# GLU steps on pairs of column blocks that share a 512-column PSUM bank, on one Trainium2 core

## The chip, the core and the metric

The kernel runs on one core of one Trainium2 chip. The engines meant below are TensorE (PE, its weight loads PEld), VectorE (DVE), ScalarE (ACT), GpSimd (POOL) and the DMA queues. The metric is device time in microseconds (us) of one execution. The time before is the median of three runs.

## The reference

```python
def _attn_ref(x):                                   # x [8, 3072, 256]
    return np.fft.fft(np.fft.fft(x, axis=1), axis=2).real.astype(np.float32)

def _moe_ref(x, w_gate, w1, w2):                    # tokens N = 24576, D = 256, E = 8, F = 1024
    # every token goes to one expert, greedily by descending logit, cap N // E tokens each
    ...
    for e in range(E):
        mask = assigned == e
        h = np.maximum(x[mask] @ w1[e], 0.0)
        out[mask] = h @ w2[e]

def _moe2_ref(x, w_a, w_b, w_out):                  # w_a, w_b [256, 1536], w_out [1536, 256]
    return ((x @ w_a) * (x @ w_b) @ w_out).astype(np.float32)
```

The three are chained: the FFT's output goes through the experts, and theirs through the last layer, called the GLU here.

## The kernel before

First comes the FFT over sequence and features (`fft_phase`). Then 48 **superblocks** of 512 tokens run, six per expert. Superblock `sb` starts with eight groups of expert products, `first(f)` into a PSUM tile `mm`, then ACT's `hH`, DVE's `hL`, and `second(f)` into two tiles `acc`. Behind them, in the same superblock, stands the GLU of superblock `sb - 1`. All products use float16 high and low halves, three matmuls for one product.

The GLU writes both `x wa` and `x wb` as Winograd's seven products on halves of features and tokens. Its loop runs over `f` = 0 to 11, blocks of 128 columns. For one `f`:

- `p1` makes tile A (`mm`); ACT copies it twice, to `u` (scaled) and to `w`. `p6` makes tile B (`acc`); DVE adds it to `u`. `p5` makes tile D (`mm`); DVE's `v = w + D`.
- `p2` adds to A; ACT copies it to `c`. `p7` adds to B; DVE's `v += B`. `p3` adds to D; DVE's `u += D`, and POOL's `g[256:] = u * v`.
- `p4`, one round later, adds to B; DVE's `w += B` and `mul`: `g[:256] = c * w`.
- `high` and `low` split `g`, 512 columns, into `gH` (ACT) and `gL` (POOL); `last(f)` multiplies both by `wot` into the tiles `y`. It is written two rounds after `p1(f)`.

Every product has 256 columns (two halves of 128 tokens). Tiles A and D rotate through three PSUM banks `mm`, B through two banks `acc` (for `f` = 0 and 1 it borrows those of `y`). Each engine runs its instructions in the order in which they are written.

Side work is written in between by `tick()` (class `Side`): the routing of the next experts (tiles `cmp`, `rt_...`, products into `bank`), the split of their weights, the preparation of tokens (`prepare`), and the end of `rescale`, which makes `x1H` and `x1L` for the next GLU. A model of the engines' queues (class `Meter`) decides: a step of side work is let in while VectorE's model time is at most 0.48 us (`SLACK`) past TensorE's. The model takes 0.066 us + columns / 960 for a VectorE instruction. Token rows come by `ahead` (an indirect DMA on POOL's queue, tile `xg`), results leave by `finish` (`ysb`, then indirect DMAs).

Almost every instruction is recorded under line L637 of a helper, so the rows are told apart by tiles.

Of the kernel before, what the change touches and what calls it, by code (L numbers as in the profile page):

```python
# [24 lines left out]
F32 = mybir.dt.float32  # L25
F16 = mybir.dt.float16
BF16 = mybir.dt.bfloat16
I32 = mybir.dt.int32
# [22 lines left out]
def shape_constants():  # L51
# [20 lines left out]
    for h in range(2):  # L72
# [23 lines left out]
        np.eye(128),  # L96
# [11 lines left out]
    below = np.stack([t <= t2, (t >= 64) & (t + 64 <= t2)], 1)       # rows t and t + 64 of the prefix sums  # L108
# [20 lines left out]
FEATURES = np.r_[0:128, 255:127:-1]      # feature at each position of a stored row  # L129


# ---------------------------------------------------------------- FFT over sequence and features
def fft_phase(tc, nc, x, wg, cd, xs, L, tick, done):
    """X = Re FFT2(x), by batch. Row n = 32 p + m of x sits on partition p = 2 a + ro, n = 64 a + 32 ro + m.
    First a DFT over a with twiddles (the product also brings the features onto partitions), then the
    DFT over the features on the sums and differences of features d and 256 - d, then the DFT over r."""
    with ExitStack() as ctx:
# [61 lines left out]
        def stage1(b, g):  # L199
            """rows m = 4 g .. 4 g + 3"""  # L200
# [93 lines left out]
# ---------------------------------------------------------------- routing: greedy by logit, with capacities  # L294
class Router:
    """Experts close in the order in which the descending greedy fills them. phase() finds the next
    one: the largest value T at which some open expert has as many unassigned tokens (by their best
    open expert) as it has room for. The search goes over the order-preserving integer image of
    float32, four bits a round. Generators: 'p' comes before tensor-engine work on fresh data."""

    def __init__(s, tc, nc, L, cd, pool, work, psum):
# [7 lines left out]
        sq = const("sq", [128, 4, 128])  # L309
        s.ident, s.samek, s.sel0, s.sel1 = [sq[:, i] for i in range(4)]  # L310
# [15 lines left out]
        s.rhs = []  # L326
        for i in range(2):
            t = pool.tile([128, NT + 4], F16, name=f"rhs{i}")
            nc.vector.tensor_copy(t[:, NT:], s.pcol)
            s.rhs.append(t)  # L330
# [18 lines left out]
    def choose(s, sl, pen=True):  # L349
        """every token's best open expert: the logit, its number, the number as one-hot"""  # L350
# [24 lines left out]
    def count(s):  # L375
        """D: by threshold (and tile) the tokens at or over it, by expert"""
# [37 lines left out]
    def phase(s, number, last):  # L414
        nc = s.nc
        est = s.tmp([128, 1], name="est")          # 8 - expert
# [28 lines left out]
        for r in range(8):  # L445
# [23 lines left out]
            if r == 0:  # L469
                # the bits of the bracket's lower end: of the integer, then of the float it stands for  # L470
# [46 lines left out]
        # the expert's tokens over T, and as many of the ties as it has room for  # L517
# [6 lines left out]
    def compact(s, j, gi, si):  # L524
        """rows to gather (gi) and token numbers (si) of the closing expert's CAP tokens"""
# [3 lines left out]
        for g in range(CAP // 512):  # L529
# [29 lines left out]
            # batch = floor(col / KS), by rounding at 2^23  # L559
# [137 lines left out]
def pow2_scales(nc, work, m, k, inv, scale):  # L697
    """inv = 2^floor(log2 m) * 2^-k, scale = 1/inv: m*scale in [2^k, 2^(k+1))"""
# [11 lines left out]
def fft_moe_glu_kernel(ctx, tc, x, wg, w1, w2, wa, wb, wo, cd, out):  # L710
# [16 lines left out]
    nc.scalar.dma_start(ki, cd["ints"])  # L727

    id16 = keep.tile([128, 128], BF16, name="id16")
    nc.vector.tensor_copy(id16, R.ident)  # L730

    unread = []

# [646 lines left out]
```

## Time and profile before

| | |
|---|---|
| median of three runs | 3851.84 us (3850.18 to 3852.17) |
| span of the profiled execution | 3846.4 us |
| PE busy in it | 3593.1 us, 93% |
| DVE busy | 3168.7 us, 82% |
| POOL busy | 2034.1 us, 53% |
| ACT busy | 1831.1 us, 48% |

The page's times are those of one profiled execution, and its span is the time from its first to its last instruction; the profiled execution has no time of its own beside this span, so the 5.4 us between span and median are taken as what lies around it. A matmul of 256 columns is drawn with some 0.27 us, but the next one starts 0.11 us later: a busy TensorE is not one at its peak, and a short stall behind a matmul doesn't show as idle time.

### The profile page before, as it was taken

The numbers are of one execution on the slowest core, as the hardware profiler recorded it, in microseconds if no ns is written. First come the engines' busy times: TensorE is split into PE (matmuls) and PEld (weight loads), VectorE is DVE, ScalarE is ACT, GpSimd is POOL, SyncE is SP. The second block draws the span as 40 slices with busy tenths as digits, with TensorE's granted clock in tenths as the row PEclk, the third lists the DMA queues.
The fourth block names the chain that finished last, engine by engine and source line by source line (L and its number), as shares of the span: only waits on it lengthen the run. The fifth ranks groups of instructions, "written<-read, shape, count | busy, mean of one in ns | idle before, by whom it ended". The sixth has DMA issues, their size and how long they took to land.

```text
span 3846.4 us, 75545 instructions
## 1 busy us (share of the span) xinstructions
PE 3593.1 (93%) x27819; PEld 2668.8 (69%) x27819; DVE 3168.7 (82%) x7867; ACT 1831.1 (48%) x4590; POOL 2034.1 (53%) x2367
## 2 busy tenths in 40 slices
PE   7998389999999999999999999999999999999998
PEld 7876256766776777667767766767667667776767
DVE  5677889899889988998999899878967797676766
ACT  2444244454445445444544454445455545545544
POOL 3333645654655555555555654655556555555545
PEclk9999599999999999999999999999999999999999
DMA  6665111101011001001100110011010000111000
GB/s 171 164 173 147 34 28 29 40 23 28 19 44 28 20 21 49 21 23 27 43 25 23 44 24 23 23 45 23 23 50 23 26 20 23 29 23 28 23 18 12
DMA packets 183636, 159.67 MB, mean 42 GB/s; under 512 B 110720, under 2 KB 159808, under 8 KB 181216
## 3 DMA queue, kind: packets, MB, share of 16 engines
q1 hardware_dynamic: 132224, 63.45, 7.1%
q0 software_dynamic: 23616, 76.57, 6.1%
q10 hardware_dynamic: 27424, 14.81, 1.8%
q8 instruction: 218, 3.57, 0.4%
q14 instruction: 154, 1.26, 0.1%
HBM read 79.29 MB, written 50.33 MB: 34 GB/s over the span
## 4 chain that ended last, share of the span: by engine, by line
PE 53%; DVE 30%; issue 7%; ACT 5%; POOL 3%; DMA 1%; ACTq 0%; DVEq 0%; POOLq 0%
PE mm L637 18%; PE acc L637 15%; PE y L637 11%; DVE u L637 4%; DVE v L637 4%; DVE g L637 3%; DVE cmp L637 3%; PE u L637 3%; PE bank L637 2%; DVE x1L L637 2%; DVE w L637 2%; ACT gH L637 2%; PE d L637 2%; PE s L637 2%; DVE hL L637 2%
## 5 line engine op out<-in xcount | busy, mean ns | idle before, releaser
L1160 POOL TENSOR_TENSOR gL<-g,gH 128x512 f16<-128x512 f32 x575 | 677.6, 1178 | 866.2 <-ACT gH L637 852.4
L637 PE MATMUL y<-wot,gH 128*128 128x256 f16 x4608 | 847.2, 273 | 2.6 <-ACT gH L637 2.6
L637 PE MATMUL y<-wot,gL 128*128 128x256 f16 x2304 | 629.8, 273 | 35.3 <-POOL gL L1160 33.7
L637 PEld LDWEIGHTS <-wst 128*128 128x128 f16 x5184 | 506.4, 98 | 123.9 <-issue 64.0
L1141 POOL TENSOR_TENSOR g<-u,v 128x256 f32<-128x256 f32 x576 | 454.4, 789 | 252.9 <-DVE u L637 190.8
L637 ACT ACTIVATE c<-mm 128x256 f32<-128x256 f32 x576 | 221.4, 384 | 686.4 <-PE mm L637 683.1
L637 PEld LDWEIGHTS <-gH 128*128 128x128 f16 x4608 | 444.7, 98 | 65.9 <-ACT gH L637 3.6
L637 ACT CAST gH<-g 128x512 f16<-128x512 f32 x577 | 355.7, 617 | 240.2 <-DVE g L637 193.1
L637 PE MATMUL mm<-xT,w1H 128*128 128x512 f16 x1536 | 460.3, 381 | 8.6 <-DMA xT<-xhl 8.6
L637 PE MATMUL mm<-x1H,wat 128*128 128x256 f16 x2304 | 439.7, 273 | 0.0
L637 ACT ACTIVATE hH<-mm 128x512 f16<-128x512 f32 x384 | 228.8, 596 | 408.1 <-PE mm L637 349.6
L637 PEld LDWEIGHTS <-wbt 128*128 128x128 f16 x3456 | 337.1, 98 | 89.1 <-issue 41.8
L637 PEld LDWEIGHTS <-wat 128*128 128x128 f16 x3456 | 336.1, 98 | 89.5 <-issue 2.7
L637 DVE TENSOR_TENSOR g<-c,w 128x256 f32<-128x256 f32 x576 | 365.6, 635 | 6.1
L637 DVE SCALAR_TENSOR_TENSOR hL<-mm,hH 128x512 f16<-128x512 f32 x384 | 262.9, 687 | 127.7 <-ACT hH L637 127.7
L637 PE MATMUL acc<-x1H,wst 128*128 128x256 f16 x1920 | 366.3, 272 | 0.0
L1207 POOL DMA_INDIRECT out_dram<-ysb,si x192 | 202.3, 1054 | 248.4 <-ACT ysb L637 207.6
L637 ACT ACTIVATE u<-mm 128x256 f32<-128x256 f32 x576 | 218.6, 380 | 227.2 <-PE mm L637 225.5
L637 PE MATMUL mm<-x1L,wat 128*128 128x256 f16 x1152 | 314.0, 273 | 0.9 <-ACT w L637 0.7
L637 PE MATMUL acc<-x1L,wst 128*128 128x256 f16 x960 | 261.4, 272 | 43.5 <-DVE u L637 43.5
L637 PEld LDWEIGHTS <-gL 128*128 128x128 f16 x2304 | 224.9, 98 | 107.8 <-POOL gL L1160 78.9
L637 PE MATMUL acc<-hL,w2H 128*128 128x512 f16 x768 | 290.9, 379 | 9.4 <-DVE hL L637 9.2
(241 smaller groups left out, 8338.6 us busy)
## 6 DMA issues: line engine op xcount, KB each, us to landing
xt<-in_x_dram SPq DMA_DIRECT2D x64, 384.0 KB, 5.5
xs<-XO SPq DMA_DIRECT2D x24, 384.0 KB, 3.2
xs<-XO ACTq DMA_DIRECT2D x48, 192.0 KB, 4.9
dwin<-in_moe_w_a_dram POOLq DMA_DIRECT2D x12, 256.0 KB, 4.7
dwin<-in_moe_w_b_dram POOLq DMA_DIRECT2D x12, 256.0 KB, 4.9
dwin<-in_moe_w_out_dram POOLq DMA_DIRECT2D x12, 256.0 KB, 3.3
xg<-xs,gi POOLq DMA_INDIRECT x192, 2.8
out_dram<-ysb,si POOLq DMA_INDIRECT x192, 2.5
```

The source lines that it names most:

```text
L637: r = f(*args, **kw)
L1141: nc.gpsimd.tensor_mul(t["g"][:, 256:], t["u"], t["v"])
L1160: nc.gpsimd.tensor_sub(gL, g, gH)
L1207: st = nc.gpsimd.indirect_dma_start(out=out, out_offset=bass.IndirectOffsetOnAxis(ap=si[:, c:c + 1], axis=0), in_=ysb[:, i], in_offset=None)
```

## The change

The loop runs over `q` = 0 to 5, pairs of column blocks. `products` fills both halves of a 512-column bank, three matmuls each of 256 columns as before, and every copy, sum and product behind it handles 512 columns in one instruction. `u * v` is written back into `u` and `c * w` into `c`. `high` and `low` now split `c` (tiles `gH0`, `gL0`, both blocks, first token half) and `u` (`gH1`, `gL1`) one by one, and `last` takes one token half `h` at a time: half 1 one round after its pair, half 0 two rounds after. `tick()` is called after nearly every step, eleven times in a full round; before, it was five times per `f`. B borrows a bank of `y` for `q` = 0 alone.

```diff
-        def product(self, dst, name, f, start=False):
+        def products(self, dst, name, F, start=False):
             i = self.X[name]
...
+            for n in range(2):
+                for w, v in ((0, self.L), (0, self.H), (1, self.H)):
+                    nc.tensor.matmul(dst[:, n * 256:n * 256 + 256], ab_part(name, w, 2 * F + n), v[:, i], start=start,
+                                     stop=(w == 1), skip_group_check=True)
+                    start = False
...
+        def p1(self, F):
+            t = self.t[F] = {n: ring.tile([128, 512], F32, name=n, bufs=1 if n == "v" else 2) for n in "uvwc"}
+            t["A"] = pmm.tile([128, 512], F32, name="mm", bufs=3)
+            self.products(t["A"], "A11", F, True)
...
-            nc.gpsimd.tensor_mul(t["g"][:, 256:], t["u"], t["v"])
...
+            nc.gpsimd.tensor_mul(t["u"], t["u"], t["v"])
...
-            nc.vector.tensor_mul(t["g"][:, :256], t["c"], t["w"])
...
+            nc.vector.tensor_mul(t["c"], t["c"], t["w"])
...
+            t["H", h] = ring.tile([128, 512], F16, name="gH%d" % h, bufs=2 - h)
+            t["L", h] = ring.tile([128, 512], F16, name="gL%d" % h, bufs=2 - h)
+            nc.scalar.copy(t["H", h], t["cu"[h]])
...
+            (eng or nc.gpsimd).tensor_sub(t["L", h], t["cu"[h]], t["H", h])
...
+        for q in range(6 if G else 0):
+            G.p1(q)
             tick()
...
+            if q == 0 and more:
+                second(6)
+                tick()
+            G.p6(q)
+            if q > 0:
+                G.high(q - 1, 1)
+                G.low(q - 1, 1)
+                tick()
+                G.p4(q - 1)
+                G.mul(q - 1)
+                tick()
+            if q > 1:
+                G.last(q - 2, 0, (0,))
+                tick()
+                G.last(q - 2, 0, (1,))
+                tick()
+            G.p5(q)
+            tick()
...
+            G.p2(q)
             tick()
...
+            if q > 0:
+                G.high(q - 1, 0)
+                G.low(q - 1, 0)
+            G.p7(q)
...
+            if q > 0:
+                G.last(q - 1, 1, (0,))
+                tick()
+                G.last(q - 1, 1, (1,))
+                tick()
+            G.p3(q)
             tick()
```

Around it, small constants change: `ones` is one column that is broadcast, `id16` comes from `ident16` (the float32 identity is no longer loaded), `rhs` of the routing has one buffer, not two, and some one-column tiles have fewer. Comments are removed. The number of matmuls is the same.

Three places show how instructions move. The first is VectorE's queue inside the GLU loop of a late superblock, without side work; before, for one block `f` (twelve of these in a superblock):

```order
L637 SCALAR_TENSOR_TENSOR u<-acc,u 128x256
L637 TENSOR_TENSOR w<-w,acc 128x256
L637 TENSOR_TENSOR v<-w,mm 128x256
L637 TENSOR_TENSOR g<-c,w 128x256
L637 TENSOR_TENSOR v<-v,acc 128x256
L637 SCALAR_TENSOR_TENSOR u<-mm,u 128x256
```

and now, for one pair (six of these):

```order
L634 SCALAR_TENSOR_TENSOR u<-acc,u 128x512
L634 TENSOR_TENSOR w<-w,acc 128x512
L634 TENSOR_TENSOR c<-c,w 128x512
L634 TENSOR_TENSOR v<-w,mm 128x512
L634 TENSOR_TENSOR v<-v,acc 128x512
L634 SCALAR_TENSOR_TENSOR u<-mm,u 128x512
```

Half as many instructions stand there, each of twice the columns, and `c * w` goes back into `c`.

The second is POOL's queue in the part of the GLU loop in which the rows of a later superblock are fetched (`xg`); before:

```order
L1160 TENSOR_TENSOR gL<-g,gH 128x512
L991 DMA xg<-xs,gi 128x256
L1141 TENSOR_TENSOR g<-u,v 128x256
L1160 TENSOR_TENSOR gL<-g,gH 128x512
L991 DMA xg<-xs,gi 128x256
```

and now (`gL` first from `u`, then from `c`):

```order
L1142 TENSOR_TENSOR u<-u,v 128x512
L1162 TENSOR_TENSOR gL_42795<-u,gH_42794 128x512
L1162 TENSOR_TENSOR gL_42834<-c,gH_42833 128x512
L989 DMA xg<-xs,gi 128x256 x2
L1142 TENSOR_TENSOR u<-u,v 128x512
```

Both fetches of a round stand together, between the second `gL` of a pair and the product `u * v` of the next.

The third is VectorE's queue in the GLU loop of a superblock that carries one round of the routing's search (four `cmp`); before:

```order
L637 TENSOR_TENSOR v<-v,acc 128x256
L637 SCALAR_TENSOR_TENSOR u<-mm,u 128x256
L637 TENSOR_TENSOR cmp<-v,rt_th 128x768
L637 SCALAR_TENSOR_TENSOR u<-acc,u 128x256
L637 TENSOR_TENSOR w<-w,acc 128x256
L637 TENSOR_TENSOR v<-w,mm 128x256
L637 TENSOR_TENSOR g<-c,w 128x256
L637 TENSOR_TENSOR v<-v,acc 128x256
L637 SCALAR_TENSOR_TENSOR u<-mm,u 128x256
L637 TENSOR_REDUCE am_31786<-rmx 128x1
L637 TENSOR_TENSOR cmp<-v,rt_th 128x768
```

and now:

```order
L634 SCALAR_TENSOR_TENSOR u<-mm,u 128x512
L634 TENSOR_TENSOR cmp<-v,rt_th 128x768
L634 SCALAR_TENSOR_TENSOR u<-acc,u 128x512
L634 TENSOR_TENSOR w<-w,acc 128x512
L634 TENSOR_TENSOR c<-c,w 128x512
L634 TENSOR_TENSOR cmp<-v,rt_th 128x768
L634 TENSOR_TENSOR v<-w,mm 128x512
L634 TENSOR_TENSOR v<-v,acc 128x512
L634 TENSOR_TENSOR cmp<-v,rt_th 128x768
L634 SCALAR_TENSOR_TENSOR u<-mm,u 128x512
L634 TENSOR_TENSOR cmp<-v,rt_th 128x768
```

All four `cmp` of a round now lie within one pair's steps; before, there was one to a block, and the other two of the round follow in the next two blocks.

Counted over superblocks 1 to 46 in VectorE's queue, 33 superblocks before hold a full load of routing or weight splits, one (number 33) a part, 12 at most two such instructions. Now 28 hold a full load, three a part, and 15 at most two.

## Rows read from the trace of the kernel before

**Rows 1.** The page: the span.

```profile
span 3846.4 us, 75545 instructions
```

**Rows 2.** Stretches: length, busy PE, PEld, DVE, ACT, POOL, clock, DMA share, GB/s.

```profile
498.50:3720.80 3222.30, 3095.43 (x24388) 2266.06 (x24389) 2740.15 (x6871) 1597.66 (x3899) 1762.32 (x2028) 1.00 0.11 28
1286.50:1644.60 358.10, 340.98 (x2750) 249.94 (x2749) 324.96 (x829) 176.14 (x427) 197.56 (x222) 1.00 0.10 29
3260.10:3326.20 66.10, 65.17 (x496) 47.81 (x494) 45.39 (x103) 33.17 (x84) 36.19 (x44) 1.00 0.10 25
3656.70:3720.80 64.10, 64.10 (x495) 48.14 (x493) 42.95 (x103) 33.12 (x84) 32.41 (x40) 1.00 0.08 18
3720.80:3846.40 125.60, 112.61 (x918) 88.59 (x916) 74.03 (x180) 49.91 (x122) 62.25 (x78) 0.98 0.04 14
```

**Rows 3.** Waits of PE in five superblocks, 1286.5 to 1644.6: total, times, longest.

```profile
PEld L637 <- POOL gL L1160: 9.2, 18, 1.0
PE acc L637 <- DVE u L637: 4.9, 5, 1.5
PE y L637 <- POOL gL L1160: 4.3, 14, 0.8
PEld bank L637 <- DVE rt_D L637: 2.4, 4, 1.0
PE acc L637 <- DVE v L637: 2.0, 4, 0.8
```

**Rows 4.** Timeline of quiet superblock 40: start, us, engine, line, operation, [idle before <-releaser].

```profile
3312.28 0.73 POOL L1141 TENSOR_TENSOR g<-u,v 128x256 f32<-128x256 f32 x1
3312.30 1.00 DVE L637 TENSOR_TENSOR g<-c,w 128x256 f32<-128x256 f32 x1
...
3314.09 1.16 POOL L1160 TENSOR_TENSOR gL<-g,gH 128x512 f16<-128x512 f32 x1 [1.08 <-ACT gH L637]
...
3314.29 1.24 DVE L637 SCALAR_TENSOR_TENSOR x1L<-xr,rs,x1H 128x256 f16<-128x256 f32 x1
...
3314.74 0.38 PE L637 MATMUL y<-wot,gH 128*128 128x256 f16 x2
...
3315.30 0.28 PE L637 MATMUL y<-wot,gL 128*128 128x256 f16 x1 [0.18 <-POOL gL L1160]
...
3315.45 0.41 DVE L637 SCALAR_TENSOR_TENSOR u<-acc,u 128x256 f32<-128x256 f32 x1
...
3315.79 0.40 DVE L637 TENSOR_TENSOR w<-w,acc 128x256 f32<-128x256 f32 x1
```

**Rows 5.** Routing's own products (tile bank) in the five superblocks: busy time.

```profile
1286.50:1644.60 358.10, 19.12 (x287) 3.08 (x20) 18.23 (x95) 0.90 (x2) 1.00 0.10 29
```

**Rows 6.** Groups by form, whole span: count | busy us, mean ns | idle before.

```profile
L637 DVE SCALAR_TENSOR_TENSOR u<-acc,u 128x256 f32<-128x256 f32 x480 | 199.3, 415 | 83.2 <-ACT u L637 77.8 <-PE acc L637 3.7 <-ACT w L637 1.1
L637 DVE SCALAR_TENSOR_TENSOR hL<-mm,hH 128x512 f16<-128x512 f32 x384 | 262.9, 687 | 127.7 <-ACT hH L637 127.7
L637 DVE TENSOR_TENSOR g<-c,w 128x256 f32<-128x256 f32 x576 | 365.6, 635 | 6.1
L637 DVE TENSOR_TENSOR cmp<-v,rt_th 128x768 f16<-128x768 f32 x196 | 228.5, 1196 | 0.0
...
L637 ACT COPY xr<-acc 128x512 f32<-128x512 f32 x96 | 56.3, 586 | 58.2 <-PE acc L637 58.0
...
L1160 POOL TENSOR_TENSOR gL<-g,gH 128x512 f16<-128x512 f32 x575 | 677.6, 1178 | 866.2 <-ACT gH L637 852.4 <-PE acc L637 9.4 <-PE mm L637 4.3
L1141 POOL TENSOR_TENSOR g<-u,v 128x256 f32<-128x256 f32 x576 | 454.4, 789 | 252.9 <-DVE u L637 190.8 <-PE y L637 51.6 <-DVE rt_w L637 6.6
L991 POOL DMA_INDIRECT xg<-xs,gi x192 | 197.1, 1027 | 54.2 <-DVE rt_w L637 17.7 <-DVE gi L637 6.7 <-issue 4.8
```

**Rows 7.** Timeline: two 512-column VectorE steps in a row, and a product's reader.

```profile
3072.68 1.28 DVE L637 SCALAR_TENSOR_TENSOR hL<-mm,hH 128x512 f16<-128x512 f32 x2
...
2400.34 0.38 PE L637 MATMUL mm<-x1H,wat 128*128 128x256 f16 x2
...
2400.76 0.38 ACT L637 ACTIVATE u<-mm 128x256 f32<-128x256 f32 x1 [0.88 <-PE mm L637]
```

More of the change, by code (lines that the diff above doesn't have):

```diff
@@ L307, in const @@
             return t
-        sq = const("sq", [128, 4, 128])
-        s.ident, s.samek, s.sel0, s.sel1 = [sq[:, i] for i in range(4)]
+        sq = const("sq", [128, 3, 128])
+        s.samek, s.sel0, s.sel1 = [sq[:, i] for i in range(3)]
         half = const("half", [128, 3, 128], F16)
@@ L325, in __init__ @@
         nc.vector.memset(s.asg, 0.0)
[L326 to L330, printed above, removed]
+        t = pool.tile([128, NT + 4], F16, name="rhs")
+        nc.vector.tensor_copy(t[:, NT:], s.pcol)
+        s.rhs = [t, t]
         s.v = pool.tile([128, NT], F32, name="v")
@@ L870, in glu_weights @@
         t = words32(wot)
-        mx = sm.tile([128, 3], F32, name="gmx")
+        mx = sm.tile([128, 3], F32, name="gmx", bufs=1)
         for c in range(3):
@@ L1130, in p2, with p7, p3 @@
             nc.scalar.activation(t["c"], t["A"], AF.Copy, scale=2.0 ** -11)
-        def p7(self, f):
-            t = self.t[f]
-            self.product(t["B"], "S3", f)
+        def p7(self, F):
+            t = self.t[F]
+            self.products(t["B"], "S3", F)
             nc.vector.tensor_add(t["v"], t["v"], t["B"])
-        def p3(self, f):
-            t = self.t[f]
-            self.product(t["D"], "S4", f)
+        def p3(self, F):
+            t = self.t[F]
+            self.products(t["D"], "S4", F)
@@ L1179, in last, with mul @@
-        def last(self, f, tiles=range(4)):
-            gH, gL, _ = self.t[f]
-            y = self.y
-            for i in tiles:
-                if f == 0 and i % 2 == 0:
-                    t = pacc.tile([128, 2, D], F32, name="y%d" % (i // 2))
-                    y += [t[:, 0], t[:, 1]]
-                sl = slice(i * 128, i * 128 + 128)
-                nc.tensor.matmul(y[i], gH[:, sl], wo_part(1, f), start=(f == 0 and i % 2 == 0), stop=False,
-                                 skip_group_check=True)
-                nc.tensor.matmul(y[i], gH[:, sl], wo_part(0, f), start=False, stop=False, skip_group_check=True)
-                nc.tensor.matmul(y[i], gL[:, sl], wo_part(0, f), start=False, stop=(f == 11),
-                                 skip_group_check=True)
+        def mul(self, F):
+            t = self.t[F]
+            nc.vector.tensor_mul(t["c"], t["c"], t["w"])
@@ new lines, in last @@
+        def last(self, F, h, ns=(0, 1), tiles=(0, 1)):
+            t, y = self.t[F], self.y
+            for n in ns:
+                f = 2 * F + n
+                for i in tiles:
+                    if f == 0 and i == 0:
+                        y.append((h, pacc.tile([128, 2, D], F32, name="y%d" % h)))
+                    dst = dict(y)[h][:, i]
+                    sl = slice(n * 256 + i * 128, n * 256 + i * 128 + 128)
+                    for g, w in (("H", 1), ("H", 0), ("L", 0)):
+                        nc.tensor.matmul(dst, t[g, h][:, sl], wo_part(w, f), start=(f == 0 and i == 0 and w == 1),
+                                         stop=(f == 11 and g == "L"), skip_group_check=True)
@@ L1250, in fft_moe_glu_kernel @@
         if pend:
-            pend.p4(11)
-            pend.mul(11)
+            pend.high(5, 1)
+            pend.low(5, 1)
+            pend.p4(5)
+            pend.mul(5)
+            tick()
+            pend.last(4, 0)
             tick()
@@ L1257, in fft_moe_glu_kernel @@
         if pend:
-            pend.high(11)
-            pend.low(11)
+            pend.high(5, 0)
+            pend.low(5, 0)
             tick()
-            pend.last(10)
+            pend.last(5, 1)
             tick()
@@ L1270, in fft_moe_glu_kernel @@
                 if pend and f == 3:
-                    pend.last(11)
+                    pend.last(5, 0)
                     pend.finish()
@@ L1283, in fft_moe_glu_kernel @@
         elif pend:
-            pend.last(11)
+            pend.last(5, 0)
             pend.finish()
@@ L1295, in fft_moe_glu_kernel @@
             next(r)
-        for f in range(12 if G else 0):
-            G.p1(f)
-            G.p6(f)
-            if f > 0:
-                G.p4(f - 1)
-            G.p5(f)
-            if f > 0:
-                G.mul(f - 1)
-            tick()
-            if f > 1:
-                G.last(f - 2, (0, 1))
-            elif more:
-                second(f + 6, (0,))
-                if f:
+        for q in range(6 if G else 0):
+            G.p1(q)
+            tick()
+            if q == 0 and more:
[16 more added lines that the diff above has]
+            tick()
+            if q == 0 and more:
+                for d in range(2):
+                    second(7, (d,))
@@ L1310, in fft_moe_glu_kernel @@
                     next(r)
+                    tick()
+            G.p2(q)
             tick()
-            G.p2(f)
-            G.p7(f)
-            if f > 0:
-                G.high(f - 1)
-                G.low(f - 1)
-            if 2 <= f < 6 and more:
-                next(r)
-            if 6 <= f < 10 and sb < NSB - 2:
-                ahead(sb + 2, f - 6)
-            tick()
-            if f > 1:
-                G.last(f - 2, (2,))
-            G.p3(f)
-            tick()
-            if f > 1:
-                G.last(f - 2, (3,))
-            elif more:
-                second(f + 6, (1,))
-                if f:
-                    next(r)
@@ L1332, in fft_moe_glu_kernel @@
-            if f == 5 and more:
-                chains.append(r)
+            if q > 0:
+                G.high(q - 1, 0)
+                G.low(q - 1, 0)
+            G.p7(q)
+            if 1 <= q < 3 and more:
+                next(r)
+                next(r)
+            if q == 3 and more:
+                chains.append(r)
+            if 3 <= q < 5 and sb < NSB - 2:
+                ahead(sb + 2, 2 * q - 6)
+                ahead(sb + 2, 2 * q - 5)
+            tick()
+            if q > 0:
+                G.last(q - 1, 1, (0,))
+                tick()
+                G.last(q - 1, 1, (1,))
+                tick()
```

96 lines of the change are left out of this document (40 added, 56 removed).

## The prediction

> **What bounds the kernel now.** The span is 3846.4 us [rows 1]; 5.4 us lie between it and the median of 3851.84. I read the busy times by stretch first, cut where a superblock's first product with w1H starts. Superblocks 1 to 46 take 3222.3 us of the span, 70.05 each [rows 2]. The reader is to compare three kinds of them. Superblock 46 (3656.7 to 3720.8), without routing and without fetches of later rows, takes 64.10 us with PE busy all the time: that is the floor of its matmuls, whose number the change leaves alone. Superblock 40 (3260.1 to 3326.2), quiet too but with four fetches on POOL's queue, takes 66.10. The five from 1286.5 to 1644.6 carry routing and take 358.10, or 71.62 each, with DVE busy 324.96, 91% [rows 2]. So TensorE bounds the kernel, and what can be gained is 2.0 us in a quiet superblock and up to 7.5 in one with routing.
>
> Next the timeline of superblock 40, for what these 2.0 us are. POOL's g (u times v) starts at 3312.28, DVE's g (c times w) at 3312.30; the latter takes 1.00 us and ends when 0.28 us have passed after POOL's. An x1L behind it takes 1.24 us, next to a gL. ACT's gH waits for g, POOL's gL for gH, and the product with gL starts at 3315.30 where, by its neighbours' spacing of 0.11, it could have at 3314.96 [rows 4]. The wait is drawn with 0.18 because the matmul before it is drawn longer than its slot. In superblocks with routing the waits list names the same chain (gL 4.3 and 9.2, two views of one wait) and DVE being late: 4.9 for u, 2.0 for v [rows 3].
>
> **The change, step by step.** *Fixed costs of DVE.* A step on 256 columns from PSUM takes 415 ns, one on 512 takes 687 [rows 6], and by starts they are 0.34 apart (3315.45, 3315.79 in [rows 4]) against 0.59 (two in 1.28 with 0.687 each, [rows 7]). So a pair saves 2 x 0.34 - 0.59 = 0.09 us of DVE's queue; a superblock has five such steps in each of six pairs, so 2.7 us. c times w took 635 ns in the mean [rows 6]; at 512 columns I take the 0.69 of the other steps plus as much waiting for POOL as before, and count no gain. ACT's copies (xr, 512 columns, 586 ns) and POOL's u times v (789 ns each of two before; one of some 1.18 as gL now, [rows 6]) save more than that, but neither engine bounds: ACT and POOL are busy 33 and 36 of 66 us [rows 2].
>
> [...]
>
> *Room before a product.* This is where the gain comes from. A step has six matmuls at 0.11 us, 0.65 us; a round has eleven steps, 7.2 us. Let p1(q) begin at 0 and follow the queue: p6 at 0.65, p4(q-1) 1.31, last of half 0 1.96 to 3.27, p5 3.27, p2 3.92, p7 4.58, last of half 1 5.23 to 6.54, p3 6.54. A reader starts 0.2 us after its step's slots end (0.04 after the drawn end of 2400.72, [rows 7]). The longest chain begins with p3's end, time 0 of the next round: DVE's u 0.2 to 0.89, POOL's u times v to 2.1, gH1 on ACT to 2.8, gL1 on POOL to 4.05 (0.69, 1.16, 0.6 and 1.16 us, [rows 4, 6]). Half 1 needs gL1 at 5.23 plus two slots, 5.45: 1.4 us of room. gL0 is ready at about 7.2 and used at 9.4. Bank B: DVE's v ends 0.9 us after p7 and p4 writes 3.3 us after it; before, the distance was 1.6. Bank D, read for v by 4.8, is written by p3 at 6.54. Each mm bank was read some 5 us before it is needed again. So nothing is tight but gL1, and the room of all others has doubled. In rounds 1 to 4, two xr (of the form of POOL's g, 0.73 undisturbed, [rows 4]) or two fetches (1.03 each, [rows 6]) stand ahead of u times v on POOL; 0.95 of these 2.1 us fill idle time, which leaves 0.3 us of room. I therefore leave a quiet superblock 0.3 us above the floor: 64.4.
>
> *DVE being late.* A round of four cmp (1196 ns each, [rows 6]) now lies inside one pair. The cmp ahead of the last u stands in 1.3 us that are free between p7 and p3, so it delays u little; one that waits for POOL makes it 0.7 late. The model lets side work in by its own time, at 0.6 us a step now instead of 0.67 for two, so what DVE saves is filled with routing at once: the order shows 28 superblocks with a full load and 3 with a part, where there were 33 and one. For a full one I add: 64.1 floor; routing's own products, at most 19.12 / 5 = 3.8 [rows 5], of which much is drawn over its neighbours, so 2.5, times 33.5 / 29.5 for the denser load, 2.8; routing's own waits (rt_D 2.4 in five, and smaller ones, [rows 3]) 1.2, unchanged; and of the remaining 71.6 - 64.1 - 2.5 - 1.2 = 3.8 us of waits in the GLU a third, 1.2. That is 69.3. The third is a choice between nothing (room always enough) and all of it (DVE as late as now).
>
> *The rest.* Fewer buffers in routing's rhs cost nothing: a compaction writes rhs a whole expert, some 350 us, after the last one read it. The smaller constants load during the first 466 us, in which nothing else moves. The last 125.6 us [rows 2] I leave unchanged.
>
> *Sum.* 28 x 69.3 + 3 x 66.5 + 15 x 64.4 = 3106 against 3222.3: 116 us less. Span 3730, time **3735 us**, 3.0% less. Partial loads stand midway.
>
> **The rivals.** *All waits in the GLU vanish.* Quiet ones 64.1, full ones 68.1, partial 65.5: 3065 us, time 3694. For it: every room but one doubles. Against: DVE stays at nine tenths in full ones.
>
> *VectorE sets the pace where routing runs.* Its own work in the five is 65.0 us each, 19.6 more than the 45.4 of a quiet one [rows 2]. Afterwards a full one holds 45.4 - 2.7 + 19.6 x 33.5 / 29.5 = 65.0. If DVE can't be busier than the 91% of now, it takes 71.6, and the kernel 28 x 71.6 + 3 x 68 + 15 x 64.4 = 3175: time 3804. For it: u and v are what PE waits for in [rows 3].
>
> *The lock between VectorE and POOL, slower.* In [rows 4] DVE steps with two SBUF inputs stand still for as long as a POOL instruction runs (1.00 and 1.24 us beside the 0.41 of u and w, which read PSUM), and 512-column instructions make each such stop up to 1.16 us. Were u 0.7 late behind a cmp that waits for gL0, fetches ahead of POOL's product (1.1) and gL1 behind a c times w (0.7), the chain's 4.05 becomes 6.5 and half 1 waits 1.05 us in that pair. It decides from (3222.3 - 3065) / (46 x 6) = 0.57 us a pair in the mean: above that the kernel is slower. At 0.8, three pairs in four fully hit, superblocks 1 to 46 take 3065 + 46 x 6 x 0.8 = 3286 and the kernel 3915. Against: quiet pairs and those with part of it have the room.
>
> [...]
>
> **How the numbers follow.** Forecast 0.57, all waits gone 0.13, VectorE's pace 0.18, slower 0.08, and 0.04 for something near no change between the last two. The range, 3675 to 3815, takes in the first three, with 20 us below the lowest for what I left in routing's own waits and the end; it leaves out the slower case and near no change. A measurement of this kernel tells a change from none at about 0.2%: faster 0.88, same 0.04, slower 0.08.
>
> **What the next profile would show.** VectorE's u, v, w on 512 columns at about 0.69 us, 288 of each kind; c from c and w between 0.69 and 1.8. Quiet superblocks near 64.4 us, fifteen of them, and full ones near 69. PE's waits for v and for u gone from quiet superblocks; those for gL only on gL1, small. Superblocks 18, 24 and 30 among the quiet ones. The prediction is wrong if PE waits for gL1 more than half a microsecond a pair, if full superblocks stay at 71 or more, or if a wait comes up where a superblock's products follow the last pair of the one before, where p4 and last stand between first(0) and first(1).

## The result and the profile after

The changed kernel takes **3811.84 us** (median of four runs, 3808.63 to 3814.82) against 3851.71 for the kernel before in the same runs: a ratio of 0.990, 95% interval 0.989 to 0.991. It is 40 us faster, not 117. The forecast of 3735 is missed by 77 us; 3811.84 lies inside the range, at its upper end.

First the stretches of the changed kernel, cut at the same places as in [rows 2] (superblocks 1 to 46, five with routing, quiet superblock 40, superblock 46, the end; columns as there):

```profile
502.80:3686.00 3183.20, 3060.24 (x24374) 2267.53 (x24375) 2536.90 (x5212) 1493.01 (x3070) 1752.47 (x1751) 1.00 0.11 28
1288.20:1646.50 358.30, 340.84 (x2831) 252.80 (x2830) 323.24 (x682) 165.16 (x336) 197.73 (x193) 1.00 0.11 29
3228.40:3294.00 65.60, 64.58 (x496) 47.98 (x494) 38.70 (x66) 31.03 (x65) 36.92 (x38) 1.00 0.10 25
3621.40:3686.00 64.60, 64.24 (x496) 48.14 (x495) 38.38 (x65) 31.26 (x65) 33.76 (x34) 1.00 0.07 18
3686.00:3812.70 126.70, 113.69 (x933) 90.18 (x930) 70.32 (x111) 45.91 (x85) 63.39 (x66) 0.98 0.04 14
```

The span is 3812.7 us. Superblocks 1 to 46 give the whole gain: 3222.3 before, 3183.2 now, where 3106 was forecast. The superblocks begin 4 us later, at 470.2 instead of 466.0, which is scatter of the FFT part: with the same order there, e5, e9, e10 and e12 begin at 465.9 to 471.0. The end is 1 us longer. Superblock 46 takes 64.6 us (64.1 before). The quiet superblock 40 went from 66.10 to 65.60 (forecast 64.4). The five with routing did not get shorter one by one; they hold more of it (368 products into `bank` against 287 in [rows 5]), and the 28 with a full load average 71.2 us (forecast 69.3).

Then the waits of TensorE over superblocks 1 to 46 of the changed kernel, the longest, and below "..." the same list for the five superblocks of [rows 3]:

```profile
PE y L634 <- POOL gL L1162: 57.3, 100, 1.4
PE bank L634 <- DVE rt_sl L634: 13.4, 8, 2.0
PE bank L634 <- DVE rt_o L634: 10.2, 13, 2.4
PE bank L634 <- DVE am L634: 10.2, 11, 1.6
PE acc L634 <- DVE u L634: 6.7, 10, 1.7
...
PE y L634 <- POOL gL L1162: 7.0, 12, 1.4
PE bank L634 <- DVE rt_o L634: 2.3, 2, 1.2
PE bank L634 <- DVE rt_sl L634: 1.4, 1, 1.4
PE acc L634 <- DVE u L634: 1.3, 2, 0.9
```

The waits for u and v, the largest of VectorE's before, are nearly gone; gL leads, and products of the routing (`bank`) follow. Since a wait behind a matmul is drawn too short (0.68 us against 0.84 by starts in the last round of superblock 41, below), I counted them by starts too: the distance from one matmul's start to the next less the usual one for its shape, wherever it is over 15 ns longer, put down to what released the later one. A wait right behind a product into `bank` is counted with the routing, whatever released it; by releaser alone u and v would have 8 us more in e2, 7 in e11, 6 in e6 and at most 1 in the others. In superblocks 1 to 46, in us (kernels in the order of their runs; "all" holds smaller kinds too):

| kernel | time | gL | GLU's u, v, w | routing's products | all | quiet superblock 41 |
|---|---|---|---|---|---|---|
| before | 3851.7 | 58 | 106 | 38 | 222 | 66.1 |
| changed | 3811.8 | 79 | 11 | 77 | 184 | 65.5 |
| e1 half 1 later | 3888.6 | 1 | 188 | 58 | 271 | 66.7 |
| e2 routing 1 us later | 3788.8 | 81 | 9 | 48 | 161 | 64.9 |
| e3 = e1 + e2 | 3858.3 | 1 | 168 | 34 | 230 | 65.8 |
| e4 less slack | 3911.0 | 42 | 0 | 210 | 282 | 64.7 |
| e5 gH for gL in half 1 | 3766.9 | 0 | 21 | 101 | 143 | 64.0 |
| e6 half 0 in between | 3933.9 | 20 | 144 | 105 | 308 | 69.5 (most quiet ones 67.9) |
| e7 before, 1 us later | 3869.2 | 65 | 101 | 43 | 242 | 66.1 |
| e8 routing 2 us later | 3792.1 | 79 | 28 | 22 | 153 | 64.9 |
| e9 chain in halves | 3782.2 | 40 | 13 | 93 | 158 | 64.8 |
| e10 halves, 2 us later | 3727.4 | 14 | 34 | 26 | 101 | 64.0 |
| e11 = e5 + e2 | 3729.6 | 0 | 23 | 54 | 106 | 64.0 |
| e12 2 us later, layers only | 3780.8 | 79 | 27 | 21 | 153 | 64.9 |

So the change did what it was said to do, 95 us less for u, v and w; 21 us came back at gL and 39 at the routing's products.

The forms that answer to [rows 6], changed kernel, whole span:

```profile
L1162 POOL TENSOR_TENSOR gL<-u,gH 128x512 f16<-128x512 f32 x287 | 386.9, 1348 | 207.9 <-ACT gH L634 207.8
L1142 POOL TENSOR_TENSOR u<-u,v 128x512 f32<-128x512 f32 x288 | 379.3, 1317 | 540.1 <-DVE u L634 319.3 <-DVE rt_w L634 71.8 <-DVE rt_ni L634 52.3
...
L634 DVE TENSOR_TENSOR c<-c,w 128x512 f32<-128x512 f32 x288 | 280.1, 973 | 11.5
...
L634 DVE SCALAR_TENSOR_TENSOR u<-acc,u 128x512 f32<-128x512 f32 x240 | 164.4, 685 | 57.3 <-ACT u L634 55.9 <-PE acc L634 1.4
```

VectorE's sums take the 0.69 us that I took. POOL's two steps of the chain take 1.32 and 1.35 in the mean, where I took 1.16 for both.

Two pieces of the timeline show the two kinds of wait. The first is the last round of quiet superblock 41, which begins with p1's matmul at 3351.32 (start, us, engine, line, operation):

```profile
3349.46 0.50 ACT L634 ACTIVATE x1H<-xr,rs 128x256 f16<-128x256 f32 x1
...
3349.86 0.61 ACT L634 CAST gH<-c 128x512 f16<-128x512 f32 x1
...
3350.55 1.25 POOL L1162 TENSOR_TENSOR gL<-c,gH 128x512 f16<-128x512 f32 x1 [1.04 <-ACT gH L634]
...
3351.30 1.18 DVE L634 SCALAR_TENSOR_TENSOR x1L<-xr,rs,x1H 128x256 f16<-128x256 f32 x2
3351.32 0.27 PE L634 MATMUL mm<-x1L,wat 128*128 128x256 f16 x1
...
3351.95 0.99 POOL L989 DMA_INDIRECT xg<-xs,gi  x1 [0.15 <-issue]
...
3352.41 0.68 DVE L634 SCALAR_TENSOR_TENSOR u<-mm,u 128x512 f32<-128x512 f32 x1
...
3353.25 1.05 POOL L989 DMA_INDIRECT xg<-xs,gi  x1 [0.30 <-issue]
...
3354.31 1.28 POOL L1142 TENSOR_TENSOR u<-u,v 128x512 f32<-128x512 f32 x1
...
3354.70 1.45 DVE L634 TENSOR_TENSOR c<-c,w 128x512 f32<-128x512 f32 x1
...
3355.62 0.62 ACT L634 CAST gH<-u 128x512 f16<-128x512 f32 x1 [1.91 <-POOL u L1142]
...
3356.32 1.24 POOL L1162 TENSOR_TENSOR gL<-u,gH 128x512 f16<-128x512 f32 x1 [0.73 <-ACT gH L634]
...
3357.62 0.28 PE L634 MATMUL y<-wot,gL 128*128 128x256 f16 x1 [0.68 <-POOL gL L1162]
```

u is ready at 3353.09, but the second fetch holds POOL until 3354.30; then u times v, gH and gL follow without a gap, and TensorE waits 0.68 us by the drawn ends, 0.84 by starts. Beside POOL's product, c times w takes 1.45 us; the 18 in superblocks 1 to 46 that overlap nothing on POOL take 0.69 each. It ends 0.56 us after POOL's product, so by these two numbers at most 0.13 of its 0.69 us of work was done beside it, an estimate.

The second is VectorE in superblock 10, which carries a compaction of the routing:

```profile
1155.28 1.32 DVE L634 TENSOR_SCALAR rt_o<-c_iota,rt_bb 128x512 f16<-128x512 f16 x1
1156.64 0.75 DVE L634 SCALAR_TENSOR_TENSOR rt_o<-c_iota,rt_bb,rt_o 128x512 f16<-128x512 f16 x1
1157.31 0.33 DVE L634 TENSOR_SCALAR rt_sl<-c_small 128x1 f32<-128x1 f32 x4
1157.44 0.11 PEld L634 LDWEIGHTS <-rt_o 128*128 128x128 f16 x2 [2.49 <-DVE rt_o L634]
1157.44 0.34 PE L634 MATMUL bank<-rhs,rt_o 128*128 128x196 f16 x2 [2.00 <-DVE rt_sl L634]
```

The product reads `rt_o`. It stands so early in TensorE's queue that all of TensorE waits 2.00 us for VectorE to make it; the model takes 0.066 us + 512 / 960 = 0.60 for a step that took 1.32 here, next to a gL on POOL (0.35 in the median of its 48). This is a wait of the order of writing, not of the products behind it.

### The profile page after: what moved, and what is told of

Same layout as the page of the kernel before. It is cut to its first block, busy times and chain, and to the rows that moved or that the text cites. A ratio compares the mean times of both kernels' runs of the same rounds, so it can differ in the third digit from the quotient of the medians.

```text
span 3812.7 us, 71013 instructions
## 1 busy us (share of the span) xinstructions
PE 3562.7 (93%) x27819; PEld 2674.9 (70%) x27819; DVE 2965.2 (78%) x6138; ACT 1722.8 (45%) x3725; POOL 2024.7 (53%) x2078
## 4 chain that ended last, share of the span: by engine, by line
PE 46%; DVE 21%; POOL 15%; issue 11%; ACT 6%; DMA 1%; ACTq 0%; POOLq 0%; DVEq 0%
PE mm L634 16%; PE acc L634 12%; PE y L634 10%; POOL gL L1162 5%; POOL u L1142 4%; POOL xg L989 3%; ACT gH L634 3%; PE u L634 3%; DVE v L634 2%; DVE u L634 2%; DVE cmp L634 2%; PE bank L634 2%; DVE rt_w L634 2%; DVE c L634 2%; PE s L634 2%
## 5 line engine op out<-in xcount | busy, mean ns | idle before, releaser
L634 PE MATMUL y<-wot,gH 128*128 128x256 f16 x4608 | 794.6, 273 | 5.2 <-ACT gH L634 5.2
L1142 POOL TENSOR_TENSOR u<-u,v 128x512 f32<-128x512 f32 x288 | 379.3, 1317 | 540.1 <-DVE u L634 319.3
L1162 POOL TENSOR_TENSOR gL<-c,gH 128x512 f16<-128x512 f32 x287 | 347.8, 1212 | 285.9 <-ACT gH L634 285.0
L1162 POOL TENSOR_TENSOR gL<-u,gH 128x512 f16<-128x512 f32 x287 | 386.9, 1348 | 207.9 <-ACT gH L634 207.8
L634 ACT ACTIVATE u<-mm 128x512 f32<-128x512 f32 x288 | 171.9, 597 | 541.4 <-PE mm L634 477.3
L634 PE MATMUL mm<-x1H,wat 128*128 128x256 f16 x2304 | 409.0, 273 | 0.0
L634 PE MATMUL acc<-x1H,wst 128*128 128x256 f16 x1920 | 340.5, 273 | 0.0
L634 ACT CAST gH<-u 128x512 f16<-128x512 f32 x288 | 178.1, 618 | 309.1 <-POOL u L1142 305.4
L634 PE MATMUL mm<-xT,w1L 128*128 128x512 f16 x768 | 292.4, 381 | 0.0
L634 PE MATMUL acc<-hH,w2L 128*128 128x512 f16 x768 | 291.0, 379 | 0.0
```

The source lines that it names most:

```text
L634: r = f(*args, **kw)
L1142: nc.gpsimd.tensor_mul(t["u"], t["u"], t["v"])
L1162: (eng or nc.gpsimd).tensor_sub(t["L", h], t["cu"[h]], t["H", h])
```

## The experiments

Three theories of the missing 77 us were to be told apart. **Chain**: u, u times v, gH and gL of half 1 are too slow for the place of their products. **Placement**: the routing's products stand too early. **Pace** (the second rival on record): VectorE, busy nine tenths where routing runs, bounds those superblocks whatever else is mended. The expectations speak of 18 quiet superblocks; it was 15, as the order had shown (18, 24, 30, 33 to 36, 39 to 46), so 18 x 1.5 = 27 us in their sums should read 14 x 1.5 = 21 (superblock 46, without fetches, waits less). The kernel before, measured beside each round of experiments, stayed at 3850.9 to 3852.4 us, so times of different rounds can be compared.

**e1: half 1 behind the third sums.**

```diff
+            G.p3(q)
+            tick()
             if q > 0:
                 G.last(q - 1, 1, (0,))
                 tick()
                 G.last(q - 1, 1, (1,))
                 tick()
-            G.p3(q)
-            tick()
```

> The changed kernel (3811.8 us) with the last products of the first half of a pair, which read gL, moved behind the third sums of the round: between the call for gL on GpSimd and its reading lie 6.8 to 7.4 us of products in place of 5.4. Waits for gL are 79 us in superblocks 1 to 46 of the changed kernel. Chain theory (what is missing of the forecast is, for two thirds, the chain of u, u*v, gH, gL): these waits go in all superblocks, 3737 us. Pace theory (VectorE sets the time of every superblock with a full load of routing, so a wait taken away there comes back at another instruction): only the 18 quiet superblocks gain 1.2 to 1.5 us each, 3785 to 3792 us. Nothing gained at all (3812) would mean that the products behind the swap wait for VectorE's u of the third sums earlier.

Measured: 3888.6 us, ratio 1.009 (1.008 to 1.011) to before. The waits for gL are gone (79 to 1), and 188 us stand at v and u. The timeline of a quiet superblock, 41, shows why there:

```profile
3421.04 1.16 POOL L1162 TENSOR_TENSOR gL<-u,gH 128x512 f16<-128x512 f32 x1 [0.73 <-ACT gH L634]
...
3421.41 1.07 DVE L634 SCALAR_TENSOR_TENSOR x1L<-xr,rs,x1H 128x256 f16<-128x256 f32 x1 [0.54 <-ACT x1H L634]
...
3422.40 0.68 DVE L634 TENSOR_TENSOR v<-w,mm 128x512 f32<-128x512 f32 x1
...
3423.13 0.27 PE L634 MATMUL mm<-x1L,wst 128*128 128x256 f16 x1 [1.06 <-DVE v L634]
```

An `x1L` of the side work stands ahead of v on VectorE; it waits 0.54 us for ACT, then runs 1.07 beside gL. The third sums write onto the bank that v has to read first, and without half 1 in between they meet this lateness. None of the three outcomes on record came; the only one that pointed this way named u, not v. The edit took away a distance between v and the third sums that the changed kernel has, so it doesn't tell what the chain alone costs.

**e2: the routing's products later.** In `Side.fits`, for steps that come before a product:

```diff
-            return at + 0.28 <= t["pe"]
+            return at + 1.28 <= t["pe"]
```

> The changed kernel with one number of the order changed: the routing's products are let into TensorE's queue 1 us of modelled time later than now (1.28 us behind the modelled end of what they read, 0.28 now). Their waits are 77 us in superblocks 1 to 46, 38 before the change. Placement theory (the routing's products now stand too early in TensorE's queue, because VectorE runs later than the model says and the GLU's waits that used to hide it are gone): these waits fall to 20 to 30 us and nothing takes their place, 3755 to 3765 us. Pace theory: the time of the full superblocks does not change, the waits move to u, v or gL or the routing spreads over more superblocks, 3800 to 3815 us.

Measured: 3788.8 us, 0.984 (0.982 to 0.986); 23 us faster than the changed kernel. The routing's products wait 48 us instead of 77, gL stays at 81. Placement is a cause, by at most half of what I gave it. The edit does more than its name says: the same rule lets in the product at the end of `rescale` (`ram`, also into `bank`), which every superblock has. In superblock 41 of e2 it comes later, ScalarE makes gH of half 0 ahead of `x1H` (at 3324.14 and 3324.65), and gL1 of the last round waits 0.21 us instead of 0.84. So superblocks without routing, too, fall from 65.5 to 64.9 us: in the ten that are quiet in both kernels this is 6 of the 23 us, and it belongs to the chain.

**e3: both edits.**

> The two edits together: half 1 of the last products behind the third sums, and the routing's products let in 1 us later. Chain and placement theories together: the two gains add, 3685 to 3700 us. Pace theory: little more than the quiet superblocks' gain, 3780 to 3792 us.

Measured: 3858.3 us, 1.002 (1.001 to 1.003). That is a miss for both theories, as e1 was. Against e1 the waits fell at the routing's products (58 to 34) and at u and v (188 to 168), 44 us by the two profiles, which lie 42 us apart; the medians lie 30 us apart, because e3's profiled execution, 3850.0 us, is the shortest of ten (up to 3861.9).

**e4: less slack.**

```diff
-SLACK = 0.48
+SLACK = 0.0
```

> The changed kernel with the slack that lets side work hold VectorE behind TensorE at 0 in place of 0.48 us of modelled time: less of the routing fits into one superblock and it takes more superblocks, with the same work in all. Pace theory (VectorE, busy 90 to 91% of the full superblocks, bounds them): the load per superblock falls, so waits fall nearly everywhere at once and the quiet superblocks become fewer, 3730 to 3760 us. Placement theory: the routing's products are let in by the same rule against the same modelled ends and go on waiting, 3785 to 3812 us. Chain theory: gL's waits are the same, 3790 to 3812 us.

Measured: 3911.0 us, 1.016 (1.014 to 1.018). The test went wrong in a way that no theory had: with so little let in, the routing fell behind, and what was due was written at once, in one or two superblocks of every six. One of them:

```profile
1151.50:1241.90 90.40, 75.41 (x621) 56.29 (x619) 64.56 (x145) 32.48 (x67) 40.41 (x40) 0.89 0.14 42
```

90.4 us with VectorE at 71%: TensorE stood still for 15 us. Its granted clock was 1.00 up to 1206, and lower in the two stretches of 10 us below "..."; the line above it is the 3 us before it fell:

```profile
1203.00:1206.00 3.00, 0.35 (x6) 0.23 (x6) 3.00 (x3) 0.80 (x2) 1.69 (x1) 1.00 0.01 3
...
1200.00:1210.00 10.00, 5.42 (x54) 4.20 (x52) 7.49 (x11) 1.72 (x3) 3.13 (x3) 0.80 0.00 1
1210.00:1220.00 10.00, 4.41 (x41) 3.57 (x40) 4.82 (x26) 0.61 (x2) 1.96 (x2) 0.50 0.12 22
```

0.50 was granted from 1206.1 to 1226.5 (from 1220 to 1230 the mean is 0.67, then 1.00 again); in the 3 us before, TensorE had worked for 0.35 us. Superblocks in which nothing was forced took 65 to 69 us. It neither supports nor hurts the pace theory.

**e5: nobody waits for gL of half 1.** The leave-out moves nothing; the low part of half 1 is missing from its output, as in e11:

```diff
-                        nc.tensor.matmul(dst, t[g, h][:, sl], wo_part(w, f), ...
+                        nc.tensor.matmul(dst, t["H" if h else g, h][:, sl], wo_part(w, f), ...
```

> The changed kernel (3811.8 us) in which the last products of the u*v half read gH a second time in place of gL; gL is still computed on GpSimd, but nobody waits for it, so the low part of that half is missing from the output. Nothing is moved, so no other wait gets less room than now. Chain theory (the 79 us of waits for gL in superblocks 1 to 46 are time lost on the path): 3733 to 3745 us, and quiet superblocks of 64.0 to 64.3 us in place of 65.5. Pace theory (in superblocks with routing VectorE would be waited for elsewhere): only the 18 quiet superblocks gain, 1.4 us each, 3785 to 3790 us, with the full ones still at 71 us.

Measured: 3766.9 us, 0.978 (0.977 to 0.980); 45 us faster than the changed kernel, between the two expectations. Quiet superblocks take 64.00 us, PE busy all the time:

```profile
3255.90:3319.90 64.00, 64.00 (x495) 48.21 (x494) 38.61 (x68) 31.02 (x65) 36.01 (x39) 1.00 0.10 26
```

So in quiet superblocks the chain is all that was left: 14 x 1.5 = 21 us. In loaded ones 58 us of waits for gL went and only 24 us of time: routing's products rose from 77 to 101, u, v and w from 11 to 21. This is the pace theory's picture in the loaded superblocks, but also that of a product that stands too early: the time that TensorE no longer waits for gL, it waits at the next routing product. e11 tells them apart.

**e6: half 0 ahead of the third sums.** As e1 from the third round on, and `last(q - 2, 0)` moved from behind `mul` to between `p7` and `p3`:

```diff
             G.p7(q)
...
+            if q > 1:
+                G.last(q - 2, 0, (0,))
+                tick()
+                G.last(q - 2, 0, (1,))
+                tick()
             G.p3(q)
             tick()
+            if q > 1:
+                G.last(q - 1, 1, (0,))
+                tick()
+                G.last(q - 1, 1, (1,))
+                tick()
```

> The changed kernel with all its work, the last products of half 1 behind the third sums as in the first experiment, but from the third round on the products of half 0, now between the calls for w and v, take their old place ahead of the third sums. So gL of half 1 gets 2.6 us more, and the third sums, which write onto what VectorE's v has to read first, keep their distance. If the first experiment failed only because that distance was lost (v then waited for 174 us): waits for v under 20 us and for gL under 20 us, 3735 to 3755 us. If any earlier third sums meet a late v in superblocks with routing: v still 80 us and more, 3800 to 3850 us. Pace theory: 3780 to 3792 us.

Measured: 3933.9 us, 1.022 (1.020 to 1.023), a miss on every line. v is indeed well (10 us at the third sums); the waits moved one place on:

```profile
PE acc L634 <- DVE u L634: 117.6, 85, 2.9
```

p7 adds onto the bank that VectorE's first u of the round has to read, and half 0 had kept it away from p6. In a round of eleven steps each of the two blocks of last products covers a distance of its own; moving either uncovers it.

**e7: the control on the kernel before**, with the edit of e2.

> Control: the kernel before (3851 us) with the same one number as in the second experiment, the routing's products let into TensorE's queue 1 us of modelled time later. The changed kernel gained 23 us by it. If the GLU's waits of the kernel before hid the early products (38 us of waits there, 77 after the change): 3840 to 3855 us, no or little gain. If the number is simply a better one whatever the GLU does: 3825 to 3832 us, the same gain as in the changed kernel.

Measured: 3869.2 us, 1.005 (1.003 to 1.006). It got slower: its routing's products wait 43 us, 38 without the edit, and its fourth superblock, where routing fell due, takes 92.4 us instead of 72.2. That is the whole loss: the other 45 superblocks together take 3149.8 us, 3150.1 without the edit. So the later products bring nothing there; in the changed kernel they bring 23 us although the fourth superblock pays there too (79 us in e2, 84 in e12 and e10, 70 without).

**e8: 2 us later**, 2.28 in the line of e2.

> The changed kernel with the routing's products let in 2 us of modelled time later than now (2.28 us, where the second experiment had 1.28 and 3788.8 us). Placement theory: the waits of the routing's products, 48 us at 1.28, fall to about 25 us, 3765 to 3775 us. If VectorE's pace is what is left: the waits only change their names, 3785 to 3795 us. If the later products push the routing behind its due dates, so that a rest of it is written at once ahead of an expert's first superblock, as with less slack: over 3800 us, with superblocks of over 80 us.

Measured: 3792.1 us, 0.985 (0.983 to 0.986). Superblocks 1 to 46 gained 8 us more than in e2 (3152.5 against 3160.4), but the rule holds beside the FFT too, and the superblocks began at 478.5 us, 8 later than in the changed kernel (470.2) and 14 later than in e2 (464.6). This is the 3785 to 3795 us of the pace theory by its number; the waits that the placement theory spoke of did fall, to 22 us.

**e9: the chain of half 1 unpaired.** u times v, gH1 and gL1 go in two steps of 256 columns:

```diff
-            nc.gpsimd.tensor_mul(t["u"], t["u"], t["v"])
+            for n in range(2):
+                sl = slice(n * 256, n * 256 + 256)
+                nc.gpsimd.tensor_mul(t["u"][:, sl], t["u"][:, sl], t["v"][:, sl])
...
-            nc.scalar.copy(t["H", h], t["cu"[h]])
+            for sl in (slice(0, 256), slice(256, 512)) if h else (slice(0, 512),):
+                nc.scalar.copy(t["H", h][:, sl], t["cu"[h]][:, sl])
...
-            (eng or nc.gpsimd).tensor_sub(t["L", h], t["cu"[h]], t["H", h])
+            for sl in (slice(0, 256), slice(256, 512)) if h else (slice(0, 512),):
+                (eng or nc.gpsimd).tensor_sub(t["L", h][:, sl], t["cu"[h]][:, sl], t["H", h][:, sl])
```

> The changed kernel (3811.8 us) with the pairing undone in the chain of the u*v half alone: u*v on GpSimd, gH on ScalarE and gL on GpSimd go as two steps of 256 columns each, so that the first column block's gL is ready about 1 us earlier; all six sums stay paired. Chain theory: most of the 79 us of waits for gL go, and with the rate of the leave-out (79 us of waits gone gave 45 us) 3775 to 3785 us, quiet superblocks 64.3 to 64.8 us. If the doubled steps hold GpSimd, and through it VectorE's c*w, as long as they save: 3805 to 3820 us.

Measured: 3782.2 us, 0.982 (0.981 to 0.984), the time that the chain theory had; of the waits for gL, half went and not most. POOL pays for it, and it can:

```profile
L1166 POOL TENSOR_TENSOR gL<-u,gH 128x256 f16<-128x256 f32 x574 | 468.8, 836 | 0.8 <-ACT gH L634 0.6
L1144 POOL TENSOR_TENSOR u<-u,v 128x256 f32<-128x256 f32 x576 | 463.6, 828 | 527.3 <-DVE u L634 309.9 <-DVE rt_w L634 71.8 <-DVE rt_ni L634 50.7
```

That is 932 us of POOL instead of 766, for a first column block that is ready earlier. Waits for gL halve (79 to 40), and routing's products take 16 of the 39 (77 to 93).

**e12 and e10: the square.** The 2 us of e8 only while the superblocks run, not beside the FFT, with everything paired (e12) and with the halves of e9 (e10):

```diff
-            return at + 0.28 <= t["pe"]
+            return at + (0.28 if s.slack == EARLY else 2.28) <= t["pe"]
```

> The last corner of a square: the changed kernel with the routing's products 2 us later beside the layers only, and everything paired. Known are the changed kernel with neither (3811.8 us), with halves alone (3782.2 us) and with both (3727.4 us). If the two causes add: 3727 + 30 = 3757 us. If they hide one another, so that TensorE's wait at a routing product gives gL its time and a wait for gL gives the routing its time: 3772 to 3782 us, so that each alone brings about 30 to 38 us and both together 84. If the delay alone carries the gain: 3727 to 3740 us.

> The same halves, and the routing's products let in 2 us of modelled time later beside the layers only (beside the FFT as now). If the two causes add: about 3812 - 33 (chain) - 33 (products: 3792.1 with the FFT's start late by 8 to 14 us) = 3740 to 3760 us. If VectorE's pace in the full superblocks takes back one for the other: 3765 to 3780 us.

Measured: e12 3780.8 us, 0.982 (0.980 to 0.983); **e10 3727.4 us, 0.967 (0.966 to 0.969)**, below its expectation, and the fastest kernel here. Halves alone bring 29.6 us, later products alone 31.1, both 84.5: each cause hid part of the other, as e12's second case had it. The waits of TensorE in e12, and below "..." in e10, superblocks 1 to 46:

```profile
PE y L634 <- POOL gL L1162: 56.1, 109, 1.6
PE acc L634 <- DVE v L634: 9.5, 7, 1.4
...
PE acc L634 <- DVE hL L634: 11.4, 14, 1.3
PE mm L634 <- DVE v L634: 10.7, 17, 1.9
PE acc L634 <- DVE v L634: 9.3, 7, 1.4
PE y L634 <- POOL gL L1166: 7.2, 18, 0.9
```

Without the early products gL stands alone at the head (e12), as without gL the products did (e5). With both treated, nothing over 11.4 is left.

**e11: e5 and e2 together.**

> The leave-out (gH read in place of gL in the u*v half, 3766.9 us) together with the routing's products 1 us later (3788.8 us alone). If chain and placement are two causes that add: 3812 - 45 - 23 = 3744 us, near the 3735 us of the forecast. If they hide one another (a product that waits gives gL its time, and the other way about): more than 23 us for the second, 3715 to 3740 us. If VectorE's pace remains: 3755 to 3767 us.

Measured: 3729.6 us, 0.968 (0.967 to 0.970), so the second edit brings 37 us here and 23 alone. For the pace theory the loaded superblocks decide: two of them in e11, and below "..." two with as much VectorE work in the changed kernel:

```profile
913.18:982.63 69.45, 66.37 (x549) 49.84 (x547) 66.74 (x118) 31.59 (x65) 39.67 (x39) 1.00 0.10 24
1256.88:1327.27 70.39, 66.99 (x527) 49.06 (x525) 67.10 (x131) 31.50 (x65) 40.23 (x39) 1.00 0.09 24
...
1148.01:1218.13 70.12, 65.86 (x503) 48.36 (x501) 66.21 (x149) 31.48 (x65) 36.74 (x39) 1.00 0.09 24
1362.09:1435.10 73.01, 67.36 (x518) 49.25 (x516) 66.07 (x151) 39.43 (x76) 39.87 (x40) 1.00 0.17 51
```

VectorE is 96 and 95% busy in the first two, 94 and 90% in the others: 91% is no ceiling, and 66 to 67 us of its work lie in 73 us or in 69.5.

## Why the prediction was wrong

*Right.* TensorE bounds the kernel; VectorE's sums take 0.69 us; u, v and w stop being waited for (106 to 11 us); the load goes to 28 full, 3 partial and 15 quiet superblocks, and 18, 24 and 30 are quiet; superblock 46 and the end stay within 0.5 and 1.1 us. VectorE's single steps are longer beside POOL's (c times w 973 ns in the mean and 2.17 us at most, where I had 1.8; 0.69 where POOL is idle), but the slower case did not come. That such a step stands still for all of POOL's instruction was my reading of the starts and lengths in [rows 4]; no run shows more than these. One of the prediction's own signs of being wrong did: full superblocks at 71 us or more.

*The first step that failed: the room of gL1*, "1.4 us of room", "0.3" with fetches. It was missing in three of the five rounds that use gL1 (by starts 0.52, 0.12 and 0.84 us in rounds 1, 4 and 5 of superblock 41), and a quiet one takes 65.5 instead of 64.4. In the last round, by its terms: u times v starts 3.0 us into the round, where my sequence had 2.0. gL0 ends at 3351.80, 0.5 us after the round began, where I had it ready at its start: an `x1H` of the side work (3349.46) stands ahead of its gH on ScalarE, a term that I had put at nothing, and in e2, where it stands behind, 0.6 us of the wait is gone. And the two fetches have gaps of 0.15 and 0.30 us in front of them that I had left out. (u itself is 0.9 us late, behind two `x1L` on VectorE, but this lies under the fetches.) Then POOL's product takes 1.28 us, and I had taken gL's 1.16; gL1 takes 1.24, not 1.16. In round 1 there are no products of half 0, 1.3 us that I had counted into every round. With gL taken out of the way (e5) a quiet superblock is at 64.0, so nothing else was missed there. This is 14 x 1.1 = 15 us of the 77.

*The second: "routing's own waits 1.2, unchanged"*. They went from 38 us to 77, which is 39 us over some 31 superblocks, 1.3 each. The products of the routing are put into the queue by a model in which VectorE is faster than it is (a `cmp` 0.066 us + 768 / 960 = 0.87, where it takes 1.14 in the mean). e7 shows that letting them in later brings nothing before the change, e2, e8 and e12 that it does after (with a part of the gain in the chain, as said at e2). e5 and e9 show the mechanism: wherever a wait of the GLU is taken away, with the routing as it was, routing's waits grow (77 to 101, 77 to 93). A TensorE that waits in the GLU gives VectorE time to reach the routing's operands; the change took that time away. That the waits for u and v had covered them in the same way in the kernel before is inferred from this, not run by itself; that the new places of `tick()` moved the products to earlier places is a second reading of the step from 38 to 77, and no run tells the two apart.

*The third: "a third" of the waits in the GLU, 1.2 a full superblock.* For u, v and w it was less, some 0.4; for gL it was 58 us over 31 loaded superblocks, 1.9 each. So the sum of a full one is off by about 1.1 for the GLU and 1.3 for the routing, and, by difference, 0.5 of that is won back elsewhere: 71.2 instead of 69.3, 53 us of the 77. The three partial ones (17, 23 and 29) take 69.3 us each instead of 66.5 and hold the rest. (Midway between 64.4 and 69.3 would have been 66.9; this slip is 1 us of the sum.)

*The rival that came nearest in time*, VectorE's pace (3804), has the wrong mechanism: its 71.6 us for a full superblock is what was measured (71.2), but by 91% as a ceiling, which e11's superblocks at 96% refute. That the result lies inside the range is luck: its upper end was drawn for this rival. The superblocks were long because TensorE waited at two kinds of places, each of which covered for the other; that is why one experiment after another gave 20 to 45 us, and only both together (e10, e11) the forecast's level.

*What stays open.* Later products also spread the routing over more superblocks (9 of e12's 46 take under 66.75 us, 15 of the changed kernel's), so their gain is not the shorter waits at `bank` alone; nor is it routing alone, since the product of `rescale` moved with them. The parts were not separated. What e10 has left, among it the fourth superblock, 83.8 us, where routing falls due, was not pursued.

## What to carry to other kernels

A wait that is removed from the engine that bounds the kernel gives time back only down to the next thing that had been late behind it: list what else was late and covered, above all side work that a model puts into the queue, and retune its margin after the change, not before. Pairing steps paid here where an instruction's fixed cost (a sum takes 0.69 us for 512 columns, 0.41 for 256) or a buffer's turnaround counts (waits for u, v and w fell from 106 to 11 us), and cost where a chain of dependent steps runs across engines: there the chain in halves was 30 us faster while the sums stayed paired. An experiment that moves one block of an in-order queue measures every distance that the block had covered, so a leave-out that moves nothing is the cleaner test.

## What was not expected of the hardware

Two 256-column steps in place of one of 512 cost POOL 1.66 us for u times v against 1.32 (828 ns each), and 1.67 for gL1 against 1.35, both in mixed company; where the step is not held up the difference is smaller (0.73 each in [rows 4] against 1.28). VectorE at 96% busy over a whole superblock of e11 still let TensorE run at 66.4 of 69.5 us. In e4 a stall of TensorE was followed by 20 us at a granted clock of 0.50 (what these cost was not separated); in superblocks 1 to 46 of the changed kernel, whose waits come singly, it was 1.00 in the mean.
